# Norm of the second MLP in the transposed layout, with statistics taken behind the first MLP and sent to all partitions by transfers

## The chip, the cores and the metric

The kernel runs on 1 core of one Trainium2 chip. The metric is device time of one execution in microseconds: before the change the median of three runs is 1674.12 us (1673.66 to 1674.39). The engines are TensorE (PE in the rows; PEld is its weight load), VectorE (DVE), ScalarE (ACT), GpSimd (POOL) and SyncE (SP), which here only issues transfers.

## The reference

A linear attention, a token-and-channel mixer and a normalized MLP follow each other; batch 8, 576 tokens, width 512 (8 heads of 64), hidden widths 256 (tokens), 1536 and 2048 (channels).

```python
q_s = softmax(q, over d); k_s = softmax(k, over tokens)
x = q_s @ (k_s.T @ v)                    # per head, heads side by side: [8, 576, 512]
h = relu(x.T @ w_tok1) @ w_tok2          # mixing over tokens
u = x + h.T
y = u + relu(u @ w_ch1) @ w_ch2          # first MLP, 512 -> 1536 -> 512
mu, var = mean(y), mean((y - mu) ** 2)   # per token, over the 512 channels
xn = (y - mu) / sqrt(var + 1e-6) * g_ln
out = y + relu(xn @ w2_ch1) @ w2_ch2     # second MLP, 512 -> 2048 -> 512
```

The MLPs' weights are float64 in memory and are decoded on the chip; the other inputs are float32.

## The kernel before

The 4608 tokens are worked in nine blocks of 512: blocks 0 to 7 hold the first 512 tokens of a batch, block 8 holds the last 64 of all eight. Each float32 operand of the MLPs is split into two parts, hi and lo, which the matmul reads as float32r, and a product is three matmuls (`PASSES`). The kernel has two halves:

- `Phase1(j)`: the first MLP of block j, in the transposed layout (channels on partitions, 512 tokens as columns). Per hidden chunk f of 12: `L1` (line 684), 12 matmuls of 512 columns, then `L2` of the chunk two steps earlier (line 701), 12 more. The attention of the next batch (`Unit`) runs between them. At the end, `finish` makes yT (4 x 128 channels by 512 tokens, buffer `y` of `main`), and `y_store` turns it back, 128 tokens at a time: 4 transposes on TensorE, a copy by ScalarE, a transfer to `y_dram`.
- `Phase2(j)`: the second MLP of block j. Per hidden chunk f of 16: `L1` (line 829) with xT, then `L2` (line 844). `Norm(j)` prepares xT while the block before is worked: it loads the rows, takes mean and variance per token (lines 768, 770), the inverse root in six small instructions, subtracts and scales (793), turns the result on TensorE (804, `px`), and writes hi (809, ScalarE) and lo (810, VectorE) of xT, with g as a factor per partition. `load` fetches the rows again for the residual, and `finish` adds and stores them.

The weights of the second MLP are decoded and split by VectorE, ScalarE and GpSimd (lines 100 to 130) in the last two blocks of the first half and the first block of the second; `loads.until` puts that work ahead of the matmuls that need it.

The order on each engine is the order of the code: `later(n, fn)` puts a piece of work n turns ahead, and `tick()` ends a turn. A chunk has four turns in the first half (one in the middle and one at the end of `L1` and of `L2`) and two in the second, so a turn there is one half step of 12 matmuls. `LAG = 2` and two buffers of `ps_hid` stand between a chunk's `L1`, its relu (ScalarE, then VectorE) and its `L2`.

Tiles of a pool lie behind each other in the order of their first use. In `main` they are ident (512 bytes of a partition), gT (16), the 12 weight tiles, h, yT, stages, xT (u), t, and then the small ones st6, mv, ve, r0 and r1 (96, 32, 16, 16, 16). The pool `att` lies behind `main`; when it is released, `w2pool` takes its place, with a stage, the weight tiles of hidden chunks 0 to 3 of the second MLP and one buffer `y` for the rows that `Norm` works on. Starts are rounded up to 32 bytes; `main` starts at a multiple of 64.

Of the kernel before, what the change touches and what calls it, by code (L numbers as in the profile page):

```python
# [16 lines left out]
P = 128  # L17
# [7 lines left out]
def kernel(  # L25
# [23 lines left out]
    nc = tc.nc  # L49
    B, H, S, D = q.shape  # L50
    DM = H * D
# [6 lines left out]
    NT = B * S  # L58
# [9 lines left out]
    BLK = 512  # L68
    NB = NT // BLK
    CT = BLK // P  # L70
    LAG = 2

    main = ctx.enter_context(tc.tile_pool(name="main", bufs=1))
# [234 lines left out]
    def later(n, fn):  # L308
        ticks.setdefault(now[0] + n, []).append(fn)
# [318 lines left out]
    def y_store(j, c):  # L628
        pt = psum("py")
        for kk in range(KD):  # L630
            nc.tensor.transpose(  # L631
                out=pt[:, kk * P:(kk + 1) * P], in_=yT_t[j][:, kk, c * P:(c + 1) * P],
                identity=ident,
            )
        if w2p:
            if c == 0:
                yn_t[j] = w2p[0].tile([P, CT, DM], F32, tag="y", name="yn")
            yn = yn_t[j][:, c]
        else:
            yn = main.tile([P, DM], F32, tag="t", bufs=2, name="yn")  # L640
        nc.scalar.activation(out=yn, in_=pt[:, 0:DM], func=AF.Copy)
        if j < B:
            dst = y_dram[j * S:j * S + S0, :].rearrange("(p c) d -> c p d", c=NC)[c]
            nc.scalar.dma_start(out=dst, in_=yn)
            return
        for i in range(P // R):
            b = c * (P // R) + i
            nc.scalar.dma_start(out=y_dram[b * S + S0:(b + 1) * S, :], in_=yn[i * R:(i + 1) * R])

    def load_ends():  # L650
        u_t[B] = main.tile([P, 2, KD, BLK], F32R, tag="u", bufs=2, name="u")
# [4 lines left out]
    class Phase1:  # L656
# [51 lines left out]
        def finish(self):  # L708
            if self.f1 < NF1:
                t = [main.tile([P, 512], F32, tag="t", bufs=2, name="part") for _ in range(2)]  # L710
                x = att.tile([P, 2, 512], F32, tag="qx", name="part")
                for dd, o in enumerate((t[0], t[1], x[:, 0], x[:, 1])):
                    nc.scalar.activation(out=o, in_=self.acc[dd], func=AF.Copy)
                for dd in range(2):
                    nc.sync.dma_start(out=part_dram[:, dd], in_=t[dd])
                nc.sync.dma_start(out=part_dram[:, 2:4], in_=x)
                return
            yT_t[self.j] = main.tile([P, KD, BLK], F32, tag="y", bufs=1, name="yT")
            yT, u = yT_t[self.j], u_t[self.j]
            for dd in range(KD):  # L720
                x = self.part[dd // 2][:, dd % 2] if self.f0 else u[:, 0, dd].bitcast(F32)
                nc.vector.tensor_tensor(out=yT[:, dd], in0=self.acc[dd], in1=x, op=ALU.add)  # L722
            def add(c):
                x = slice(c * P, (c + 1) * P)
                nc.gpsimd.tensor_tensor(  # L725
                    out=yT[:, :, x], in0=yT[:, :, x], in1=u[:, 1, :, x].bitcast(F32), op=ALU.add
                )

            for c in range(CT):
                if self.f0 == 0:  # L730
                    later(2 * c if self.j > 1 else 0, lambda c=c: add(c))
                later((5, 8, 12, 15)[c] if self.j < B - 1 else 5 + 2 * c, lambda c=c: y_store(self.j, c))
# [1 line left out]

    ln_t = {}

    def load_y(j, pool):
        y = pool.tile([P, CT, DM], F32, tag="y", name="y")
        src = y_dram[j * BLK:(j + 1) * BLK, :]
        nc.sync.dma_start(out=y, in_=src.rearrange("(p c) d -> p c d", c=CT))  # L740
        return y

    class Norm:
        def __init__(self, j):
            self.j = j

        def start(self, at, turns=12):
            def call(fn, i):
                return lambda: fn(i)

            later(at, self.load)
            for i in range(CT // 2):
                later(at + 4 + i, call(self.stats, i))
                later(at + 9 + i, call(self.hat, i))
            later(at + 6, self.root)
            later(at + 8, self.rstd)
            for kk in range(KD):
                later(at + turns + kk + kk // 2, call(self.turn, kk))

        def load(self):  # L760
            self.y = load_y(self.j, w2p[0])

        def stats(self, i):
            if i == 0:
                self.st = main.tile([P, CT, 6], F32, tag="st6", name="st6")
                self.mv = main.tile([P, CT, 2], F32, tag="mv", name="mv")
            for c in range(2 * i, 2 * i + 2):
                nc.vector.bn_stats(out=self.st[:, c], in_=self.y[:, c])
            for c in range(2 * i, 2 * i + 2):
                nc.vector.bn_aggr(out=self.mv[:, c], in_=self.st[:, c])  # L770

        def root(self):
            self.ve = main.tile([P, CT], F32, tag="ve", name="ve")
            self.r = main.tile([P, CT], F32, tag="r0", name="r0")
            nc.vector.tensor_scalar(
                out=self.ve, in0=self.mv[:, :, 1], scalar1=1e-6, scalar2=None, op0=ALU.add
            )
            later(1, lambda: nc.scalar.activation(out=self.r, in_=self.ve, func=AF.Sqrt))

        def rstd(self):  # L780
            ve, r0 = self.ve, self.r
            r1 = main.tile([P, CT], F32, tag="r1", name="r1")
            nc.vector.reciprocal(out=r0, in_=r0)
            nc.vector.tensor_tensor(out=r1, in0=r0, in1=r0, op=ALU.mult)
            nc.vector.tensor_tensor(out=r1, in0=r1, in1=ve, op=ALU.mult)
            nc.vector.tensor_scalar(
                out=r1, in0=r1, scalar1=-0.5, scalar2=1.5, op0=ALU.mult, op1=ALU.add
            )
            nc.vector.tensor_tensor(out=r0, in0=r0, in1=r1, op=ALU.mult)

        def hat(self, i):
            for c in range(2 * i, 2 * i + 2):
                nc.vector.tensor_scalar(
                    out=self.y[:, c], in0=self.y[:, c], scalar1=self.mv[:, c, 0:1],
                    scalar2=self.r[:, c:c + 1], op0=ALU.subtract, op1=ALU.mult,
                )

        def turn(self, kk):
            if kk == 0:
                self.xT = main.tile([P, 2, KD, BLK], F32R, tag="u", bufs=2, name="xT")  # L800
                ln_t[self.j] = self.xT
            pt = psum("px")
            for c in range(CT):
                nc.tensor.transpose(  # L804
                    out=pt[:, c * P:(c + 1) * P],
                    in_=self.y[:, c, kk * P:(kk + 1) * P], identity=ident,
                )
            g = gT[:, kk:kk + 1]
            nc.scalar.activation(out=self.xT[:, 0, kk], in_=pt, func=AF.Copy, scale=g)
            nc.vector.scalar_tensor_tensor(  # L810
                out=self.xT[:, 1, kk], in0=pt, scalar=g, in1=self.xT[:, 0, kk].bitcast(F32),
                op0=ALU.mult, op1=ALU.subtract,
            )

    class Phase2:
# [1 line left out]
            self.j, self.f1 = j, NF2  # L817

        def load(self):
            self.y = load_y(self.j, main)  # L820

        def L1(self, f, mid):
            xT = ln_t[self.j]
# [25 lines left out]
                    )  # L849

        def finish(self):
            y = self.y
            dst = out[self.j * BLK:(self.j + 1) * BLK, :].rearrange("(p c) d -> p c d", c=CT)
            for c in range(CT):
                nc.vector.tensor_tensor(out=y[:, c], in0=self.acc[c], in1=y[:, c], op=ALU.add)  # L855
                if self.j == NB - 1:
                    nc.sync.dma_start(out=dst[:, c], in_=y[:, c])
            if self.j < NB - 1:
                nc.gpsimd.dma_start(out=dst, in_=y)  # L859

    with tc.manual_schedule():
        spare += [
# [65 lines left out]
        for j in range(NB):  # L928
            o = Phase2(j)
            steps += [(o, f) for f in range(NF2)]  # L930

# [19 lines left out]
        for o, f in steps:  # L951
            if isinstance(o, Phase1):
# [4 lines left out]
                if f == 0:  # L957
# [3 lines left out]
                    elif o.j == B - 1:  # L961
# [13 lines left out]
                        for n in range(5, 29):  # L975
                            later(n, lambda: loads.pump(2))
                        later(20, load_ends)
                    elif o.j == NB - 1:
                        Norm(0).start(18, 15)
                if o.j <= 1:  # L980
                    loads.until(len(tok) + 4 * (f // 2) + 2)
            else:
                if o.j == 0:
                    loads.until(4 * (f // 2) + 2)
                if f == 0:
                    later(16, o.load)
                    if o.j + 1 < NB:
                        Norm(o.j + 1).start(14 if o.j == 0 else 8)
# [44 lines left out]
```

## Time and profile before

| | |
|---|---|
| median of three runs | 1674.12 us |
| the profiled execution, its span | 1673.57 us, 1671.8 us |
| TensorE, its weight load, busy | 98%, 83% |
| VectorE, ScalarE, GpSimd busy | 39%, 25%, 19% |
| mean DMA rate | 63 GB/s |

The first half lasts to about 855 us of the span, the second to the end. Starts in a timeline are in us from the span's start. Matmuls are pipelined, so the busy time of one is more than its distance from the next; the pace is read from starts.

### The profile page before, as it was taken

How to read it: one execution, taken by the hardware profiler on the slowest of the kernel's cores; microseconds unless marked ns; L12 is line 12 of the kernel's file. 1: busy time of each engine (PE TensorE's matmuls, PEld its weight loads, DVE VectorE, ACT ScalarE, POOL GpSimd, SP SyncE). 2: the span in 40 equal slices, each digit the busy share in tenths (PEclk: the TensorE clock that was granted, in tenths of full speed). 3: DMA queues.
4: the chain of work that ended last, by engine and by line, in shares of the span. 5: the costliest groups of instructions: out<-in, count | busy, mean ns of one | idle time of the engine just before them, and what ended most of it. 6: DMA issues, size and time to landing. Idle time of an engine off the chain costs nothing.

```text
span 1671.8 us, 20195 instructions
## 1 busy us (share of the span) xinstructions
PE 1642.0 (98%) x8136; PEld 1380.9 (83%) x8136; DVE 644.3 (39%) x1290; ACT 410.1 (25%) x824; POOL 318.5 (19%) x244
## 2 busy tenths in 40 slices
PE   5999999999999999999999999999999999999998
PEld 4888888888888888888888888888888888888887
DVE  6875434344333434353557621222223131222211
ACT  4663333323232323321222211111111111111110
POOL 5743522232232313221223200000000000000000
PEclk9999999999999999999999999999999999999999
DMA  8552312121121212133225210101010101010010
GB/s 230 126 159 75 87 49 69 49 53 51 42 68 28 76 36 69 28 107 114 88 86 173 76 44 25 51 25 51 25 51 25 51 17 60 0 69 8 5 46 26
DMA packets 122062, 105.39 MB, mean 63 GB/s; under 512 B 92976, under 2 KB 101424, under 8 KB 118512
## 3 DMA queue, kind: packets, MB, share of 16 engines
q1 hardware_dynamic: 115568, 86.27, 17.9%
q10 hardware_dynamic: 5248, 9.44, 1.6%
q0 software_dynamic: 1152, 8.39, 1.2%
q8 instruction: 64, 1.05, 0.3%
q14 instruction: 30, 0.25, 0.0%
HBM read 82.05 MB, written 22.02 MB: 62 GB/s over the span
## 4 chain that ended last, share of the span: by engine, by line
PE 94%; DVE 2%; POOL 1%; issue 1%; ACT 1%; DMA 1%; SPq 0%; POOLq 0%; DVEq 0%; ACTq 0%
PE ph L829 24%; PE acc L844 24%; PE ph L684 17%; PE acc L701 17%; PE pu L601 4%; PE pg L538 3%; PE pk L514 2%; PE py L631 1%; PE px L804 1%; PE pq L559 1%; PE pq L586 1%; DMA rawq<-in_q 0%; DVE spare L138 0%; DVE dt L108 0%; POOL yT L725 0%
## 5 line engine op out<-in xcount | busy, mean ns | idle before, releaser
L142 DVE SCALAR_TENSOR_TENSOR h<-ph,h 128x512 fp32r<-128x512 f32 x252 | 174.0, 691 | 708.8 <-ACT h L141 708.7
L829 PE MATMUL ph<-xT,w 128*128 128x512 f32 x1728 | 420.2, 392 | 0.0
L844 PE MATMUL acc<-w,h 128*128 128x512 f32 x1728 | 420.0, 392 | 0.0
L829 PEld LDWEIGHTS ph<-xT,w 128*128 128x128 f32 x1728 | 323.0, 188 | 70.5 <-POOL w L130 0.2
L844 PEld LDWEIGHTS acc<-w,h 128*128 128x128 f32 x1728 | 322.9, 188 | 68.9
L141 ACT ACTIVATE h<-ph 128x512 fp32r<-128x512 f32 x252 | 150.5, 597 | 770.7 <-PE ph L829 587.0
L684 PE MATMUL ph<-u,w 128*128 128x512 f32 x1296 | 324.7, 395 | 0.0
L701 PE MATMUL acc<-h,w 128*128 128x512 f32 x1296 | 323.7, 394 | 0.0
L701 PEld LDWEIGHTS acc<-h,w 128*128 128x128 f32 x1296 | 237.1, 188 | 46.7
L684 PEld LDWEIGHTS ph<-u,w 128*128 128x128 f32 x1296 | 236.8, 188 | 46.7 <-DVE u L621 0.4
L859 POOL DMA_DIRECT2D out<-y x8 | 4.4, 556 | 635.8 <-DVE y L855 635.8
L467 POOL TENSOR_TENSOR qt<-rawq,qm 128x640 f32<-128x640 f32 x24 | 30.3, 1261 | 241.0 <-PE pt L461 95.5
L130 POOL TENSOR_TENSOR w<-t,w 128x512 fp32r<-128x512 f32 x32 | 41.9, 1310 | 152.8 <-ACT w L129 152.8
L538 PE MATMUL pg<-w,qn 128*128 128x256 f32 x480 | 63.8, 285 | 3.4 <-ACT w L137 3.4
L538 PEld LDWEIGHTS pg<-w,qn 128*128 128x128 f32 x480 | 62.0, 193 | 6.0 <-ACT w L137 3.7
L601 PE MATMUL pu<-w,hs 128*128 128x288 f32 x384 | 61.4, 295 | 0.0
L601 PEld LDWEIGHTS pu<-w,hs 128*128 128x128 f32 x384 | 54.4, 188 | 0.3 <-ACT hs L141 0.2
L138 DVE TENSOR_TENSOR qT<-pq,qT 128x512 fp32r<-128x512 f32 (+1 forms) x48 | 22.0, 458 | 76.1 <-ACT qT L137 76.1
L725 POOL TENSOR_TENSOR yT<-yT,u 128x512 f32<-128x512 f32 x32 | 43.0, 1359 | 37.9 <-DVE yT L722 37.9
L482 POOL TENSOR_TENSOR kt<-rawk,kb 128x640 f32<-128x640 f32 x24 | 38.1, 1587 | 40.8 <-ACT kb L478 40.8
L138 POOL TENSOR_TENSOR qn<-qt,qn 128x640 fp32r<-128x640 f32 x24 | 38.0, 1582 | 32.7 <-ACT qn L137 30.9
L129 ACT ACTIVATE w<-t 128x512 fp32r<-128x512 f32 x32 | 20.3, 633 | 97.0 <-DVE t L121 94.6
(140 smaller groups left out, 1243.3 us busy)
## 6 DMA issues: line engine op xcount, KB each, us to landing
y<-y_dram SPq DMA_DIRECT2D x18, 1024.0 KB, 4.8
st<-in_moe_w_ch SPq DMA_DIRECT2D x31, 512.0 KB, 3.8
vt<-in_v SPq DMA_DIRECT2D x64, 128.0 KB, 2.9
y_dram<-yn ACTq DMA_DIRECT2D x32, 256.0 KB, 2.4
out<-y POOLq DMA_DIRECT2D x8, 1024.0 KB, 4.1
rawk<-in_k SPq DMA_DIRECT2D x54, 128.0 KB, 2.8
rawq<-in_q SPq DMA_DIRECT2D x27, 256.0 KB, 3.1
stage<-in_moe_w_ch SPq DMA_DIRECT2D x10, 512.0 KB, 3.8
```

Of the source, the lines that this page charges most:

```text
L130: nc.gpsimd.tensor_tensor(out=lo, in0=x, in1=hi.bitcast(F32), op=ALU.subtract)
L138: engine.tensor_tensor(out=lo, in0=x, in1=hi.bitcast(F32), op=ALU.subtract)
L141: nc.scalar.activation(out=hi, in_=x, func=AF.Relu)
L142: nc.vector.scalar_tensor_tensor(out=lo, in0=x, scalar=0.0, in1=hi.bitcast(F32), op0=ALU.max, op1=ALU.subtract)
L482: nc.gpsimd.tensor_tensor(out=self.kt, in0=self.kr, in1=kb.to_broadcast([P, NC + 1, 2, D]), op=ALU.subtract,)
L538: nc.tensor.matmul(out=pg[:, 0:T], lhsT=self.qn[:, x, c], rhs=w1[:, y, c, :], start=(n == 0), stop=(n == len(terms) - 1),)
L601: nc.tensor.matmul(out=pu[:, 0:HN], lhsT=l, rhs=r, start=(n == 0), stop=(n == len(terms) - 1))
L684: nc.tensor.matmul(out=ps, lhsT=w[:, x, kk, fo:fo + P], rhs=u[:, y, kk], start=(n == 0), stop=(n == 3 * KD - 1),)
L701: nc.tensor.matmul(out=self.acc[dd], lhsT=w[:, x, f % 2, dd * P:(dd + 1) * P], rhs=h[:, y], start=(f == self.f0 and n == 0), stop=(f == se ...
L725: nc.gpsimd.tensor_tensor(out=yT[:, :, x], in0=yT[:, :, x], in1=u[:, 1, :, x].bitcast(F32), op=ALU.add)
L829: nc.tensor.matmul(out=ps, lhsT=w[:, x, kk, fo:fo + P], rhs=xT[:, y, kk], start=(n == 0), stop=(n == 3 * KD - 1),)
L844: nc.tensor.matmul(out=self.acc[c], lhsT=h[:, x, c * P:(c + 1) * P], rhs=w[:, y, f % 2], start=(f == 0 and n == 0), stop=(f == self.f1 - 1 ...
```

## The change

Statistics are taken in `y_store`, from the copy that ScalarE has just made, and kept in `mr`. yT is stored a second time as it stands (`yT_dram`). `Root` makes the inverse roots for seven blocks at once near the end of the first half and for the other two in block 0 of the second; it turns the table of means and inverse roots with one transpose each time and stores it to `mr_dram`. `Norm` then loads yT and, for half of the tokens at a time, mean and inverse root sent to all 128 partitions by a transfer; VectorE subtracts, GpSimd multiplies, and hi and lo of xT are made from that without TensorE. All scratch tensors have a block as their first dimension. The second half goes through the blocks in the order 0 to 6, 8, 7.

```diff
-    y_dram = dram.tile([NT, DM], F32, name="y_dram")
+    y_dram = dram.tile([NB, P, CT, DM], F32, name="y_dram")
+    yT_dram = dram.tile([NB, P, KD, BLK], F32, name="yT_dram")
+    mr_dram = dram.tile([NB, 2 * BLK], F32, name="mr_dram")
+
+    mr = main.tile([P, NB, 2, CT], F32, name="mr")
...
+        nc.scalar.dma_start(out=y_dram[j, :, c], in_=yn)
+        st = main.tile([P, 6], F32, tag="st6", bufs=2, name="st6")
+        nc.vector.bn_stats(out=st, in_=yn)
+        nc.vector.bn_aggr(out=mr[:, j, :, c], in_=st)
...
+            later(8, lambda: nc.sync.dma_start(out=yT_dram[self.j], in_=yT))
...
+    class Root:
...
+        def start(self, at):
+            for n, fn in zip((0, 1, 2, 3), (self.root, self.rstd, self.turn, self.store)):
+                later(at + 2 * n, fn)
...
+        def turn(self):
+            n = (self.j1 - self.j0) * 2 * CT
+            pm = psum("pm")
+            nc.tensor.transpose(
+                out=pm[:n, 0:P],
+                in_=mr[:, self.j0:self.j1].rearrange("p j x c -> p (j x c)"), identity=ident,
+            )
+            self.rows = main.tile([P, P], F32, tag="mrr", name="mrr")[:n]
+            nc.scalar.activation(out=self.rows, in_=pm[:n, 0:P], func=AF.Copy)
+
+        def store(self):
+            dst = mr_dram[self.j0:self.j1].rearrange("j (x p) -> (j x) p", p=P)
+            nc.sync.dma_start(out=dst, in_=self.rows)
...
+            later(at, self.load)
+            for i in range(2):
+                later(at + 4 * i, call(self.load_b, i))
+                later(at + 4 * i + 4, call(self.hat, i))
+            for kk in range(KD):
+                later(at + turns + kk + kk // 2, call(self.turn, kk))
+
+        def load(self):
+            self.y = w2p[0].tile([P, KD, BLK], F32, tag="y", name="yT")
+            nc.sync.dma_start(out=self.y, in_=yT_dram[self.j])
+
+        def load_b(self, i):
+            self.b = w2p[0].tile([P, 2, HB], F32, tag="mrb", name="mrb")
+            src = mr_dram[self.j].rearrange("(x n) -> x n", x=2)[:, i * HB:(i + 1) * HB]
+            nc.sync.dma_start(out=self.b, in_=src.partition_broadcast(P))
+
         def hat(self, i):
...
+            y = self.y[:, :, i * HB:(i + 1) * HB]
+            mu, r = (self.b[:, x:x + 1].to_broadcast([P, KD, HB]) for x in range(2))
+            nc.vector.tensor_tensor(out=y, in0=y, in1=mu, op=ALU.subtract)
+            nc.gpsimd.tensor_tensor(out=y, in0=y, in1=r, op=ALU.mult)
...
-            pt = psum("px")
-            for c in range(CT):
-                nc.tensor.transpose(
-                    out=pt[:, c * P:(c + 1) * P],
-                    in_=self.y[:, c, kk * P:(kk + 1) * P], identity=ident,
-                )
-            g = gT[:, kk:kk + 1]
-            nc.scalar.activation(out=self.xT[:, 0, kk], in_=pt, func=AF.Copy, scale=g)
+            g, y = gT[:, kk:kk + 1], self.y[:, kk]
+            nc.scalar.activation(out=self.xT[:, 0, kk], in_=y, func=AF.Copy, scale=g)
...
+        ORDER = [*range(B - 1), B, B - 1]
+        for j in ORDER:
...
+                        Root(0, B - 1).start(30)
                     elif o.j == NB - 1:
                         Norm(0).start(18, 15)
...
+                    later(18, o.load)
+                    if o.j == 0:
+                        Root(B - 1, NB).start(26)
+                    if o.j != ORDER[-1]:
+                        Norm(ORDER[ORDER.index(o.j) + 1]).start(15 if o.j == 0 else 8)
```

On TensorE in the second half, before, around the turn of a block (a row is a place in the engine's order; acc and ph are the sums of `L2` and `L1`, px the turned rows):

```order
1094 L829 MATMUL ph_8551<-xT,w 128x512 x12
1095 L804 MATMUL px<-ident,y 128x128 x4
1096 L844 MATMUL acc_8311<-w,h 128x512 x3
1097 L844 MATMUL acc_8312<-w,h 128x512 x3
1098 L844 MATMUL acc_8313<-w,h 128x512 x3
1099 L844 MATMUL acc_8314<-w,h 128x512 x3
1100 L804 MATMUL px<-ident,y 128x128 x4
1101 L829 MATMUL ph_8594<-xT,w 128x512 x12
```

and the same place now:

```order
1092 L842 MATMUL ph_8640<-xT,w 128x512 x12
1093 L857 MATMUL acc_8383<-w,h 128x512 x3
1094 L857 MATMUL acc_8384<-w,h 128x512 x3
1095 L857 MATMUL acc_8385<-w,h 128x512 x3
1096 L857 MATMUL acc_8386<-w,h 128x512 x3
1097 L842 MATMUL ph_8670<-xT,w 128x512 x12
```

The transposes between the half steps are gone, and nothing stands in their place. On VectorE, before, near the end of block 0 of the second half (lines 100 to 121 decode weights, L142 is the lo part of h, L810 that of xT):

```order
903 L121 SCALAR_TENSOR_TENSOR t<-stage_6575,t 128x512
904 L810 SCALAR_TENSOR_TENSOR xT<-px,gT,xT 128x512
905 L142 SCALAR_TENSOR_TENSOR h<-ph_8117,h 128x512
906 L100 TENSOR_SCALAR st<-st 128x512
907 L108 TENSOR_SCALAR t<-st 128x512
```

and now, with the small instructions of the second table:

```order
962 L126 SCALAR_TENSOR_TENSOR t<-stage_6656,t 128x512
963 L822 SCALAR_TENSOR_TENSOR xT<-yT,gT,xT 128x512
964 L147 SCALAR_TENSOR_TENSOR h<-ph_8186,h 128x512
965 L762 RECIPROCAL mr<-mr 128x2x4
966 L763 TENSOR_TENSOR r_8202<-mr 128x8
967 L764 TENSOR_TENSOR r_8202<-r_8202,ve 128x8
968 L765 TENSOR_SCALAR r_8202<-r_8202 128x8
969 L768 TENSOR_TENSOR mr<-mr,r_8202 128x2x4
970 L822 SCALAR_TENSOR_TENSOR xT<-yT,gT,xT 128x512
```

Behind the lo part of ph_8186 five small instructions have come in, for which TensorE's transpose of the table waits. That transpose stands behind the next group, ph_8235:

```order
1021 L842 MATMUL ph_8186<-xT,w 128x512 x12
1022 L857 MATMUL acc_7717<-w,h 128x512 x3
1023 L857 MATMUL acc_7718<-w,h 128x512 x3
1024 L857 MATMUL acc_7719<-w,h 128x512 x3
1025 L857 MATMUL acc_7720<-w,h 128x512 x3
1026 L842 MATMUL ph_8235<-xT,w 128x512 x12
1027 L773 MATMUL pm<-ident,mr 16x128
```

So two half steps lie between the group and the transpose. On SyncE's queue a block of the second half had two loads of 1 MB before (`y<-y_dram`, all blocks in one row, with the last decoded weights ahead and the last stores behind):

```order
263 L163 DMA st<-in_moe_w_ch 128x2x512
264 L163 DMA stage_6575<-in_moe_w_ch 128x2x512
265 L183 DMA st<-in_moe_w_ch 128x1024 x2
266 L740 DMA y<-y_dram 128x2048 x15
267 L857 DMA out<-y 128x512 x4
```

and has now, behind the store of the second table:

```order
279 L188 DMA st<-in_moe_w_ch 128x1024 x2
280 L782 DMA mr_dram<-mrr 16x128
281 L803 DMA yT<-yT_dram 128x2048
282 L808 DMA mrb<-mr_dram 128x2x256 x2
283 L833 DMA y<-y_dram 128x2048
284 L803 DMA yT<-yT_dram 128x2048
```

Two broadcasts have come between the two loads of a block, the second of them with a wait for GpSimd.

## Rows read from the trace of the kernel before

**Rows 1.** The page: busy shares, granted clock by slice, and the chain that ended last.

```profile
PE 1642.0 (98%) x8136; PEld 1380.9 (83%) x8136; DVE 644.3 (39%) x1290; ACT 410.1 (25%) x824; POOL 318.5 (19%) x244
...
PEclk9999999999999999999999999999999999999999
...
PE 94%; DVE 2%; POOL 1%; issue 1%; ACT 1%; DMA 1%; SPq 0%; POOLq 0%; DVEq 0%; ACTq 0%
```

**Rows 2.** Waits of TensorE: line, releaser, us in total, times, longest.

```profile
PE pt L433 <- DMA spare<-in_k: 5.1, 1, 5.1
PE pt L433 <- DMA rawk<-in_k: 4.5, 1, 4.5
...
```

**Rows 3.** Groups by line, the transposes: busy us, mean ns of one, idle before.

```profile
L804 PE MATMUL px<-ident,y 128*128 128x128 f32 x144 | 21.6, 272 | 0.0
```

**Rows 4.** Timeline of TensorE, one block's turn: start, us, engine, line, count.

```profile
1001.91 2.88 PE L829 MATMUL ph<-xT,w 128*128 128x512 f32 x12
1004.63 0.60 PE L804 MATMUL px<-ident,y 128*128 128x128 f32 x4
1004.99 2.99 PE L844 MATMUL acc<-w,h 128*128 128x512 f32 x12
...
1020.09 2.88 PE L829 MATMUL ph<-xT,w 128*128 128x512 f32 x12
1022.81 2.43 PE L844 MATMUL acc<-w,h 128*128 128x512 f32 x10
```

**Rows 5.** Timeline of TensorE, the first chunks of block 1.

```profile
946.80 2.95 PE L829 MATMUL ph<-xT,w 128*128 128x512 f32 x12
...
960.63 2.96 PE L844 MATMUL acc<-w,h 128*128 128x512 f32 x12
963.43 2.96 PE L829 MATMUL ph<-xT,w 128*128 128x512 f32 x12
...
985.59 2.88 PE L829 MATMUL ph<-xT,w 128*128 128x512 f32 x12
```

**Rows 6.** Timeline of TensorE, matmuls of the attention: early and in the first half.

```profile
36.72 1.87 PE L538 MATMUL pg<-w,qn 128*128 128x256 f32 x15
38.42 0.46 PE L570 MATMUL pq<-spare,qn 128*128 128x128 f32 x4
...
413.48 0.96 PE L601 MATMUL pu<-w,hs 128*128 128x288 f32 x6
414.27 1.55 PE L684 MATMUL ph<-u,w 128*128 128x512 f32 x6
```

**Rows 7.** Groups by line, elementwise work: busy us, mean ns, idle before and releaser.

```profile
L725 POOL TENSOR_TENSOR yT<-yT,u 128x512 f32<-128x512 f32 x32 | 43.0, 1359 | 37.9 <-DVE yT L722 37.9
...
L768 DVE BATCH_NORM_STATS2 st<-y 128x6 f32<-128x512 f32 x36 | 22.8, 676 | 4.9 <-DMA y<-y_dram 4.9
L855 DVE TENSOR_TENSOR y<-acc,y 128x512 f32<-128x512 f32 x36 | 22.5, 682 | 4.8 <-PE acc L844 4.8
L770 DVE BATCH_NORM_AGGREGATE mv<-st 128x2 f32<-128x6 f32 x36 | 5.4, 173 | 0.0
```

**Rows 8.** Timeline of all engines, near the end of block 0 of the second half.

```profile
925.88 0.68 DVE L115 SCALAR_TENSOR_TENSOR t<-st,t 128x512 uint32<-128x512 uint32 x1
...
928.04 1.29 POOL L130 TENSOR_TENSOR w<-t,w 128x512 fp32r<-128x512 f32 x1 [4.32 <-ACT w L129]
928.20 1.68 DVE L115 SCALAR_TENSOR_TENSOR t<-st,t 128x512 uint32<-128x512 uint32 x1
...
932.15 2.89 PE L844 MATMUL acc<-w,h 128*128 128x512 f32 x12
...
935.62 0.68 DVE L142 SCALAR_TENSOR_TENSOR h<-ph,h 128x512 fp32r<-128x512 f32 x1
```

**Rows 9.** DMA issues: transfer, queue, count, KB each, median us to landing.

```profile
y<-y_dram SPq DMA_DIRECT2D x18, 1024.0 KB, 4.8
...
rawq<-in_q SPq DMA_DIRECT2D x27, 256.0 KB, 3.1
```

More of the change, by code (lines that the diff above doesn't have):

```diff
@@ L70 @@
     CT = BLK // P
+    HB = BLK // 2
     LAG = 2
@@ L641, in y_store @@
         nc.scalar.activation(out=yn, in_=pt[:, 0:DM], func=AF.Copy)
[L642 to L648, printed above, removed]
+        nc.scalar.dma_start(out=y_dram[j, :, c], in_=yn)
+        st = main.tile([P, 6], F32, tag="st6", bufs=2, name="st6")
+        nc.vector.bn_stats(out=st, in_=yn)
+        nc.vector.bn_aggr(out=mr[:, j, :, c], in_=st)
     def load_ends():
@@ L751, in start @@
             later(at, self.load)
[L752 to L756, printed above, removed]
+            for i in range(2):
+                later(at + 4 * i, call(self.load_b, i))
+                later(at + 4 * i + 4, call(self.hat, i))
             for kk in range(KD):
@@ L760, in load @@
         def load(self):
[L761 to L776, printed above, removed]
-            )
[L778 to L789, printed above, removed]
@@ L791, in hat @@
-        def hat(self, i):
[L792 to L796, printed above, removed]
+            self.y = w2p[0].tile([P, KD, BLK], F32, tag="y", name="yT")
[4 more added lines that the diff above has]
+            nc.sync.dma_start(out=self.b, in_=src.partition_broadcast(P))
@@ L819, in load @@
         def load(self):
-            self.y = load_y(self.j, main)
+            self.y = main.tile([P, CT, DM], F32, tag="y", name="y")
+            nc.sync.dma_start(out=self.y, in_=y_dram[self.j])
         def L1(self, f, mid):
@@ L851, in finish @@
         def finish(self):
-            y = self.y
-            dst = out[self.j * BLK:(self.j + 1) * BLK, :].rearrange("(p c) d -> p c d", c=CT)
+            y, last = self.y, self.j == ORDER[-1]
+            if self.j < B:
+                dst = out[self.j * S:self.j * S + S0, :].rearrange("(p c) d -> p c d", c=CT)
+                dst = [(slice(0, P), dst)]
+            else:
+                dst = out.rearrange("(b s) d -> s b d", s=S)[S0:S]
+                n = P // R
+                dst = [
+                    (slice(i * R, (i + 1) * R), dst.rearrange("s (c i) d -> i s c d", i=n)[i])
+                    for i in range(n)
+                ]
             for c in range(CT):
                 nc.vector.tensor_tensor(out=y[:, c], in0=self.acc[c], in1=y[:, c], op=ALU.add)
[L856 to L859, printed above, removed]
+                if last:
+                    for p, x in dst:
+                        nc.sync.dma_start(out=x[:, c], in_=y[p, c])
+            if not last:
+                for p, x in dst:
+                    nc.gpsimd.dma_start(out=x, in_=y[p])
     with tc.manual_schedule():
@@ L927 @@
             steps += [(o, f) for f in range(o.f0, o.f1)]
-        for j in range(NB):
+        ORDER = [*range(B - 1), B, B - 1]
+        for j in ORDER:
             o = Phase2(j)
@@ L985 @@
                 if f == 0:
-                    later(16, o.load)
-                    if o.j + 1 < NB:
-                        Norm(o.j + 1).start(14 if o.j == 0 else 8)
+                    later(18, o.load)
[3 more added lines that the diff above has]
+                        Norm(ORDER[ORDER.index(o.j) + 1]).start(15 if o.j == 0 else 8)
             ps, n = o.L1(f, tick)
```

28 lines of the change are left out of this document (21 added, 7 removed).

## The prediction

> **What bounds the kernel now.** I read the page's busy shares and its chain first, then who TensorE waits for, then TensorE's timeline in the second half. The reader is to see that TensorE is busy for 98% of the span and carries 94% of the chain [rows 1], and that it waits for named releasers only in the front of the kernel, where q, k and v arrive: the two longest waits are 5.1 and 4.5 us [rows 2], and both are on line 433, which runs for the first eight units alone. From the middle on, the end is set by the number of TensorE instructions times their pace, and by nothing else. So an edit counts if it takes TensorE work away, changes TensorE's pace, or makes TensorE wait. Work of VectorE, ScalarE, GpSimd and the queues counts only through the third.
>
> **The transposes that go.** Each of the nine blocks of the second MLP has its normalized rows turned on TensorE: 144 transposes, 36 groups of four [rows 3]. Their busy time doesn't say what they cost, since matmuls overlap, so I take it from starts. Without a transpose, the twelve matmuls of a half step follow each other in 2.72 us (1020.09 to 1022.81) [rows 4]. The stretch from 1001.91 to 1020.09 has six such half steps and the four groups of one block: 18.18 us, where six alone take 6 x 2.72 = 16.32. One block's turn therefore costs 1.86 us, of which about 0.35 a group are the transposes (1004.63 to the next start, 1004.99) and the rest is the slower run-in of the matmuls behind them. Nine blocks: 9 x 1.86 = 16.7 us, all on the bounding engine. This is the term I am surest of.
>
> **What TensorE gets instead.** Two transposes of the table of means and deviations (line 773), one with 56 rows and one with 16. Each is at most a group of four: 1.86 / 4 = 0.47 us, and at least a quarter of the 0.35. Both together 0.2 to 0.9; I take 0.5.
>
> **A term the diff doesn't name: where the tiles lie.** The first half steps of each second-MLP block are slower with no transpose near: 960.63 to 963.43 is 2.80 us, where 2.72 is usual [rows 5]. From 946.80 to 985.59 there are 14 half steps in 38.79 us; 14 x 2.72 = 38.08, so 0.71 us a block, 6.4 us over nine. The slow half steps of both matrices are those of hidden chunks 0 to 3, whose weights lie in the pool `w2pool`; all other weights lie in `main`. In `main` the identity (512 bytes) and gT (16, rounded up to 32) come first, so every weight, xT and h tile starts 32 bytes past a multiple of 64; the small tiles at the end of `main` add 96 + 4 x 32 = 224, so `w2pool` starts on a multiple of 64. A slow matmul thus pairs a tile at 0 with one at 32, a fast one two tiles at 32. The change puts mr (9 x 2 x 4 x 4 = 288 bytes, 32 past a multiple of 64) behind gT, and its small tiles at the end come to 64 + 160 + 160 + 512 = 896, a multiple of 64. Everything then starts on a multiple of 64, `w2pool` too. How fast is a pair at 0 and 0? The attention's tiles are such pairs: six matmuls of 288 columns take 413.48 to 414.27, 132 ns each, 12 above the 120 of 288 columns at 2.4 GHz, the clock that is granted from the first slices on [rows 1, 6]. A pair at 32 and 32 takes 2720 / 12 = 226.7, 13 above the 213.3 of 512 columns; the mixed pair 233.3, 20 above. So I read the excess as that of a mismatch, which the change removes: between 0 and 6.4 us, or a loss if the reading is wrong (below). I take 6.4.
>
> The Trainium skill ("SBUF — State Buffer", section "Specifications (TRN2)") gives SBUF lines of 16 bytes, and a penalty for crossing to a new one. By that rule a start 32 bytes further on changes nothing, and this term would be zero (rival 1). The rows above show 0.08 us a half step between two places, and no run so far shows that it is the start and not the region that makes it.
>
> **VectorE, ScalarE, GpSimd.** Statistics move from the second half to the copies behind the first MLP: 36 bn_stats at 676 ns and 36 bn_aggr at 173 [rows 7], 0.85 us each pair, 3.4 a block on a VectorE that is 39% busy [rows 1]. Each waits for ScalarE's copy of that tile. Behind it stands the lo part of h, which TensorE needs four half steps (10.9 us) later; that covers it. Per block of the second MLP, VectorE loses four subtract-and-scale instructions and gets two subtractions of 1024 columns. The nearest rows are 682 ns for 512 columns of two inputs (line 855) and 680 for two inputs from SBUF (line 115) [rows 7, 8], so 1.4 us each. GpSimd gets two multiplications of 1024 columns: line 725 does 512 in 1359 ns, so 2.7 us. In a steady block the first half of the tokens is worked at turn 12 and the second at turn 16 of 32, and ScalarE starts on xT at turn 20. A turn is a half step there. From turn 16 there are 4 x 2.72 = 10.9 us for 1.4 + 2.7 = 4.1. Nothing of this is on the path.
>
> **The transfers.** A block's rows are written a second time (1 MB), loaded transposed (1 MB; 4.8 us for such a load [rows 9]) and joined by two broadcasts of 256 KB (3.1 us for the nearest load of that size, 4.8 for the upper end). On SyncE's queue the second broadcast waits for GpSimd's first product, since both use one buffer, and y for the residual is queued behind it. That delays y by the same 4.1 us at most; it is needed at the block's end, 14 turns (38 us) later. In the first half the extra store waits for GpSimd's last add, at a place where the loads ahead of it have already waited for later work of GpSimd. No cost.
>
> **The two places with little room.** Both are at the change of halves, where weights are still being decoded. (a) Block 0: its first subtraction stands on VectorE eleven turns ahead of the first xT (in the first half a turn is a quarter step, 1.4 us), but blocks VectorE until row load and broadcast have landed, and again for the second broadcast: two waits of up to 4.8 us, against a cover of three half steps (8.2 us) before TensorE needs the buffer that VectorE holds. (b) The second table: the transposition stands two half steps (5.44 us) behind the group whose lo part the last five small VectorE instructions follow. In the profile a lo part there starts 3.5 us after its group (932.15 to 935.62) and takes 0.68; five small ones add about 1: 5.1 us of 5.44. GpSimd's longer products can hold VectorE up: a step on line 115 takes 0.68 us alone and 1.68 where GpSimd works [rows 8]. Two such holds of up to 2.7 us make the upper end, 5 us; the lower end is 0. I take 1 us for both places.
>
> The Trainium skill ("SBUF — State Buffer", "Who interferes with whom") says that a VectorE instruction with two SBUF inputs and a GpSimd instruction that reads SBUF exclude each other for the whole instruction; the 1.68 agrees. By it alone each product would hold VectorE for its full 2.7 us wherever they meet, and the sum would have the 5 us in place of 1.
>
> **The sum.** -16.7 + 0.5 - 6.4 + 1.0 = -21.6 us on the profiled execution's 1673.57 us (span 1671.8 and 1.8 around it), which lies 0.55 below the median of 1674.12. On the median: 1652.5 us. Its own range is 1650 to 1657 (waits 0 to 5, the two transposes 0.2 to 0.9).
>
> **Rivals.**
> 1. The slow half steps are slow for another reason (region of memory, not start): the 6.4 stays. 1674.12 - 16.7 + 0.5 + 1 = 1659. For it: no row here has 512 columns at 0 and 0.
> 2. Pairs at 0 and 0 are faster than any now. For it: fifteen matmuls of 256 columns at 0 and 0 take 36.72 to 38.42, 113 ns each, 7 above 106.7 [rows 6]. With 7 above 213.3 for 512 columns, the 5184 matmuls of a pair at 32 and 32 would gain 6.4 ns and the 864 mixed ones 13: 33 + 11 = 44 us in place of the 6.4, and 1615. Against it: the 288-column rows, at 12. Halfway, 1634.
> 3. The other side: a start at 0 is itself what costs, 20 above the columns or more. The 512-column rows alone would bear this too, as each slow pair has a tile at 0. The 5184 matmuls that now have 226.7 would get 233.3: + 34 us, and 1674.12 + 34 - 15.2 = 1693. It decides from 15.2 / 5184 = 2.9 ns a matmul on. Against it stand the 132 ns above.
> 4. The transposes go, but TensorE waits in their place: (a) or (b) at several times their bound, or each block's two broadcasts land late. A steady block has 10.9 - 4.1 = 6.8 us of room, so it would take loads of over 11 us. With 1.2 us a block and 5 at the change of halves: 1653 + 11 + 4 = 1668.
>
> **Chances.** Forecast 0.57, rival 1 0.18, rival 2 0.12, rival 3 0.06, rival 4 0.07. The range from 1636 to 1661 holds the first two and the weaker part of the third. A measurement can tell about 0.2% (3.3 us) from no change. Faster by more: the forecast, rivals 1 and 2 and most of 4: 0.91. Slower: rival 3 with little else, 0.06. Within: 0.03.
>
> **What would show it.** Right: no transposes of px, no gap in their place, half steps of 2.72 us at all turns of a second-MLP block, so a block of 32 x 2.72 = 87.0 us; VectorE's statistics early. Wrong: half steps of 2.80 at hidden chunks 0 to 3 (rival 1), of 2.65 or less everywhere (2), of 2.80 everywhere (3), or TensorE idle before xT or line 773 (4).

## The result, and the profile after

The changed kernel takes 1659.34 us (median of four runs, 1658.92 to 1659.97), against 1674.24 us (1673.66 to 1674.39) for the kernel before in the same comparison: a ratio of 0.9912, 95% interval 0.9899 to 0.9926. That is 14.9 us faster, where 21.6 was forecast. The time lies in the wide range, 1636 to 1661, and on the figure of rival 1, whose reason turned out to be wrong. The forecast's own range, 1650 to 1657, doesn't hold it.

The page of the changed kernel: busy shares, the granted clock by slice, and the chain that ended last.

```profile
PE 1624.8 (98%) x7994; PEld 1365.8 (82%) x7994; DVE 650.0 (39%) x1230; ACT 408.5 (25%) x819; POOL 363.9 (22%) x263
...
PEclk9999999999999999999999999999999999999999
...
PE 90%; DVE 4%; DMA 1%; issue 1%; POOL 1%; ACT 1%; SPq 1%; DVEq 0%; POOLq 0%; ACTq 0%
```

Against [rows 1] TensorE has 142 instructions less (144 transposes gone, two added) and 17.2 us less of busy time. It still bounds the kernel. In the chain DVE now has 4%, where it had 2%.

Who TensorE waits for in the changed kernel (us in total, times, longest); the first two answer to [rows 2], the last two are new.

```profile
PE pt L438 <- DMA spare<-in_k: 5.4, 1, 5.4
PE pt L438 <- DMA rawk<-in_k: 4.7, 1, 4.7
...
PE ph L686 <- DVE h L147: 0.9, 1, 0.9
...
PE pm L773 <- DVE mr L768: 0.5, 1, 0.5
```

Here is where the time went, from the starts of the blocks in both traces. Seven steady blocks of the second MLP fell from 89.63 to 87.74 us each (-1.89). Its first block fell from 91.53 to 89.91. The last block of the first half, which prepares the first normalised rows and so gets rid of one turn too, fell by 0.59 only, and the block ahead of it, which holds the first table, grew by 0.75. The last block of all grew by 0.1. Five blocks of the first half, ahead of these two, became 0.4 shorter in all; why is open. The front grew by 0.75, but it differs by that much between runs of kernels that are equal there, so it isn't put down to the change. Together this is -14.2 us, by which the two profiled spans differ (1671.8 and 1657.6); the medians are 14.9 apart.

TensorE's timeline in a steady block of the changed kernel, first chunks (above "...") and a place from chunk 4 on in another block (below); it answers to [rows 4, 5].

```profile
1121.14 2.96 PE L842 MATMUL ph<-xT,w 128*128 128x512 f32 x12
1123.94 2.92 PE L857 MATMUL acc<-w,h 128*128 128x512 f32 x12
1126.70 2.96 PE L842 MATMUL ph<-xT,w 128*128 128x512 f32 x12
1129.49 2.92 PE L857 MATMUL acc<-w,h 128*128 128x512 f32 x12
...
1000.76 2.88 PE L842 MATMUL ph<-xT,w 128*128 128x512 f32 x12
1003.48 2.88 PE L857 MATMUL acc<-w,h 128*128 128x512 f32 x12
```

No transposes stand between the half steps at 1000.76, and a start follows the one before by 2.72 us. But from 1121.14 a pair of half steps still takes 5.56 us (1121.14 to 1126.70) instead of 5.44. The slow half steps of [rows 5] did not go.

The elementwise groups of the changed kernel that answer to [rows 7]: busy us, mean ns, idle before.

```profile
L649 DVE BATCH_NORM_STATS2 st<-yn 128x6 f32<-128x512 f32 x36 | 24.7, 687 | 21.1 <-ACT yn L646 21.1
...
L813 DVE TENSOR_TENSOR yT<-yT,mrb 128x1024 f32<-128x1024 f32 x18 | 24.1, 1340 | 6.0 <-DMA mrb<-mr_dram 6.0
L814 POOL TENSOR_TENSOR yT<-yT,mrb 128x1024 f32<-128x1024 f32 x18 | 43.9, 2436 | 252.5 <-issue 180.3 <-DVE yT L813 72.2
```

The sizes were about as estimated (1.4 us for VectorE's subtraction, 2.7 for GpSimd's product; 676 ns for the statistics). The broadcasts land 5.1 us behind their issue in the list of DMA issues (median of 18), above the 3.1 to 4.8 taken for them from [rows 9].

Last, all engines of the changed kernel at the one place where the first normalised block makes TensorE wait.

```profile
832.68 1.23 DVE L813 TENSOR_TENSOR yT<-yT,mrb 128x1024 f32<-128x1024 f32 x1 [2.21 <-DMA mrb<-mr_dram]
...
833.99 2.78 POOL L814 TENSOR_TENSOR yT<-yT,mrb 128x1024 f32<-128x1024 f32 x1 [3.80 <-DVE yT L813]
834.55 2.77 DVE L126 SCALAR_TENSOR_TENSOR t<-st,t 128x512 uint32<-128x512 uint32 x1
...
837.35 0.63 ACT L134 ACTIVATE w<-t 128x512 fp32r<-128x512 f32 x1 [9.70 <-DVE t L126]
837.89 1.07 ACT L146 ACTIVATE h<-ph 128x512 fp32r<-128x512 f32 x2
...
838.50 0.69 DVE L147 SCALAR_TENSOR_TENSOR h<-ph,h 128x512 fp32r<-128x512 f32 x1 [1.18 <-ACT h L146]
...
839.25 2.14 PE L686 MATMUL ph<-u,w 128*128 128x512 f32 x8 [0.93 <-DVE h L147]
```

It is read from the bottom up: TensorE needs a PSUM tile that VectorE's line 147 frees. Line 147 stands behind ScalarE's line 146, that behind ScalarE's line 134, and that behind VectorE's line 126, which takes 2.77 us beside GpSimd's product where it takes 0.69 alone.

### The profile page after: what moved, and what is told of

Same layout as the page of the kernel before. It is cut to its first block, busy times and chain, and to the rows that moved or that the text cites. A ratio compares the mean times of both kernels' runs of the same rounds, so it can differ in the third digit from the quotient of the medians.

```text
span 1657.6 us, 19945 instructions
## 1 busy us (share of the span) xinstructions
PE 1624.8 (98%) x7994; PEld 1365.8 (82%) x7994; DVE 650.0 (39%) x1230; ACT 408.5 (25%) x819; POOL 363.9 (22%) x263
## 4 chain that ended last, share of the span: by engine, by line
PE 90%; DVE 4%; DMA 1%; issue 1%; POOL 1%; ACT 1%; SPq 1%; DVEq 0%; POOLq 0%; ACTq 0%
PE ph L842 24%; PE acc L857 24%; PE ph L686 16%; PE acc L703 16%; PE pu L606 4%; PE pg L543 3%; PE pk L519 2%; PE py L636 1%; PE pq L564 1%; PE pq L591 1%; DVE t L120 1%; DMA mrb<-mr_dram 1%; DVE t L126 1%; DMA rawq<-in_q 0%; DVE spare L143 0%
## 5 line engine op out<-in xcount | busy, mean ns | idle before, releaser
L814 POOL TENSOR_TENSOR yT<-yT,mrb 128x1024 f32<-128x1024 f32 x18 | 43.9, 2436 | 252.5 <-issue 180.3
```

Source lines behind the costliest of these rows:

```text
L814: nc.gpsimd.tensor_tensor(out=y, in0=y, in1=r, op=ALU.mult)
```

## Experiments

**The transposes put back.** On TensorE alone, into a PSUM tile that nothing reads:

```
+            pt = psum("px")
+            for c in range(CT):
+                nc.tensor.transpose(
+                    out=pt[:, c * P:(c + 1) * P], in_=y[:, c * P:(c + 1) * P], identity=ident,
+                )
```

> The changed kernel with the four 128x128 transposes of each turned Norm put back on TensorE; their result is not used. Theory 'the gain is TensorE's own time for the transposes': each block gets its 1.86 to 1.89 us back, about 1675 us, level with the kernel before. Rival 'the gain came from waits that the transposes had caused': clearly less comes back, 1660 to 1668 us.

Measured: 1675.34 us, ratio to the kernel before 1.0007 (0.9997 to 1.0016). A steady block is 89.58 us again, 1.84 more than in the changed kernel. TensorE's timeline of this kernel shows the groups back at the half steps:

```profile
1006.35 0.60 PE L823 MATMUL px<-ident,yT 128*128 128x128 f32 x4
1006.70 2.99 PE L862 MATMUL acc<-w,h 128*128 128x512 f32 x12
1009.53 0.60 PE L823 MATMUL px<-ident,yT 128*128 128x128 f32 x4
```

So the gain is TensorE's own time for the transposes and for the matmuls behind them (from 1006.70 to 1009.53 it is 2.83 us instead of 2.72).

**Other weights for the slow chunks.** The weights of hidden chunks 4 to 7, whose tiles lie in `main`, are read in chunks 0 to 3 of eight of the nine blocks of the second MLP (all but block 0); so the product is another one.

```
-            w, fo = wa2[f // 2], (f % 2) * P
+            w, fo = wa2[f // 2 + 2 if f < 4 and self.j else f // 2], (f % 2) * P
```

and the same for `wb2`.

> In blocks 1 to 7 of each half where the condition holds, hidden chunks 0 to 3 read the weights of chunks 4 to 7, whose tiles lie low in SBUF, in place of their own (so the output differs from the reference; count and shape of the matmuls stay). Theory 'place of the weights': the half steps of 2.80 us in chunks 0 to 3 become 2.72 as in chunks 4 to 7, 0.64 to 0.71 us a block, about 5 us less in all: near 1654 us. Theory 'turn in the block or work beside it': half steps stay 2.80 and the time stays at 1659 us.

Measured: 1653.41 us (ratio 0.9873, 0.9856 to 0.9889). Each of the eight blocks is 0.70 us shorter; TensorE's timeline at the first chunks:

```profile
1119.59 2.88 PE L842 MATMUL ph<-xT,w 128*128 128x512 f32 x12
1122.31 2.88 PE L857 MATMUL acc<-w,h 128*128 128x512 f32 x12
```

All starts of these chunks are 2.72 us apart. It is the tiles, then, and not the turn in the block or the work that runs beside it. That left two readings: the tiles lie high in memory, or their start doesn't fit their partner's.

**A map of the memory.** Twelve tiles from 20 to 217 KB, all pairs as stationary and moving operand, nothing beside.

> A measurement by itself: nothing of the reference is computed, the output is one constant tile. Twelve tiles of 128x512 fp32r at rising addresses of SBUF (a at 20 KB of a partition, b 60, c 100, d 140, e 160, f 172, g 178, h 184, i 190, j 198, k 208, l 217), and 24 matmuls of 512 columns for each pair of a tile as stationary operand and a tile as moving one, nothing else running beside. Theory 'the address itself': a pair with one of the upper tiles takes about 233 ns a matmul and a pair of lower ones about 227, with a boundary between 182 and 185 KB. Theory 'two regions in one pair': pairs of two lower and pairs of two upper tiles take 227, mixed ones 233. Theory 'not the place at all' (the turn in the block, or what runs beside): all pairs take the same to within 1 ns.

Measured, from TensorE's timeline of this kernel (pair of the lowest tile with itself and with the highest):

```profile
13.23 5.60 PE L42 MATMUL paa<-ata 128*128 128x512 f32 x24
18.67 5.60 PE L42 MATMUL pab<-atb,ata 128*128 128x512 f32 x24
...
73.07 5.60 PE L42 MATMUL pal<-atl,ata 128*128 128x512 f32 x24
```

The second series starts 5.44 us behind the first, and so does every other: 226.7 ns a matmul, and no pair differs by as much as 0.1 ns. The height in memory costs nothing. This seems to contradict the experiment before it, until one looks at what the twelve tiles have in common: all start on a multiple of 1024 bytes.

**Both operands from the upper tiles.** In the first multiplication of chunks 0 to 3 (the same eight blocks) the moving operand is a weight tile of the upper region instead of xT.

```
-                        out=ps, lhsT=w[:, x, kk, fo:fo + P], rhs=xT[:, y, kk],
+                        out=ps, lhsT=w[:, x, kk, fo:fo + P],
+                        rhs=wb2[1 - f // 2][:, y, kk % 2] if f < 4 and self.j else xT[:, y, kk],
```

> In the later blocks the first multiplication of hidden chunks 0 to 3 takes as its moving operand a weight tile that lies high in SBUF, as its stationary one does, in place of xT, which lies low (the output differs from the reference; count and shape of the matmuls stay). Theory 'two regions in one pair': these half steps become 2.72 us, those of the second multiplication stay 2.80. Theory 'the address itself': they stay 2.80, or rise to about 2.88 if both operands pay.

Measured: one run of 1659.16 us. TensorE's timeline:

```profile
1122.34 2.89 PE L842 MATMUL ph<-w 128*128 128x512 f32 x12
1125.07 2.89 PE L858 MATMUL acc<-w,h 128*128 128x512 f32 x12
...
1133.26 2.89 PE L842 MATMUL ph<-w 128*128 128x512 f32 x12
1135.99 2.96 PE L858 MATMUL acc<-w,h 128*128 128x512 f32 x12
1138.79 2.92 PE L842 MATMUL ph<-w 128*128 128x512 f32 x12
1141.54 2.95 PE L858 MATMUL acc<-w,h 128*128 128x512 f32 x12
```

Two upper tiles together are fast: 2.73 us from 1122.34 to 1125.07 and from 1133.26 to 1135.99. An upper weight tile with the low h stays slow (1135.99 to 1138.79, 2.80), and the fast pair behind it starts slowly (2.75). A block is 0.24 us shorter; the whole time hides it, since this run's front and first half were 1.9 us longer up to the change of halves. So it takes a pair of unlike tiles, as the prediction had it. In the compiled program the lower weights, xT and h start at 192 modulo 256; the upper weights (186176 and further by multiples of 8192) start at 64. Modulo 64 both are 0, and there the prediction had stopped.

**128 bytes of room.** The changed kernel with one unused tile:

```
                         bufs[:] = [w2pool.tile([P, 512, 2], U32, name="stage3")]
+                        w2pool.tile([P, 32], U32, name="pad")
```

> The changed kernel, with 128 unused bytes of a partition ahead of the weight tiles of hidden chunks 0 to 3, nothing else. All weights, xT and h now start at 448 bytes modulo 512; before this the four upper tiles started at 320 and their partners at 448 (equal modulo 64 and 128, not modulo 256). Theory 'starts of the two operands of a matmul must agree over a longer stretch than 64 bytes': the half steps of 2.80 us in chunks 0 to 3 become 2.72, 0.64 to 0.71 us a block over nine blocks, about 6 us less: 1653 us. Theory 'high address': half steps stay 2.80, 1659 us.

Measured: 1652.71 us (ratio 0.987, 0.9855 to 0.9885). TensorE's timeline at the same chunks as above:

```profile
1118.92 2.88 PE L842 MATMUL ph<-xT,w 128*128 128x512 f32 x12
1121.64 2.88 PE L857 MATMUL acc<-w,h 128*128 128x512 f32 x12
1124.36 2.88 PE L842 MATMUL ph<-xT,w 128*128 128x512 f32 x12
```

Starts are 2.72 us apart everywhere, a steady block takes 87.04 us (32 x 2.72), and the nine blocks give back 6.3 us (0.67 in the first, 0.70 in each of the others). Only the starts of that pool's tiles moved, so the start is shown to be the cause.

**Which starts agree.** A sweep by itself.

> A measurement by itself: nothing of the reference is computed, the output is one constant tile. Sixty series of 48 matmuls of 512 columns, the stationary operand read from 0, 64, 128 or 320 bytes behind a multiple of 512, the moving one from 0 to 1024 bytes behind one (in the names of the tiles digits are written a to j, so pgexbci is stationary 64, moving 128). Theory 'starts must agree': 226.7 ns a matmul where the two differ by a multiple of 256 or 512, 231 to 235 ns where they differ by 64, 128 or 192 bytes (and by 32, as in the kernel before); the differences at which it is fast give the stretch. Theory 'it takes more than the starts': 226.7 ns for all.

Measured, TensorE's timeline with the stationary operand at 0 (`pa` + x + the moving one's bytes):

```profile
13.08 11.04 PE L44 MATMUL paxa<-mv,st 128*128 128x512 f32 x48
23.96 11.28 PE L44 MATMUL paxbg<-mv,st 128*128 128x512 f32 x48
35.08 11.37 PE L44 MATMUL paxdc<-mv,st 128*128 128x512 f32 x48
46.28 11.15 PE L44 MATMUL paxge<-mv,st 128*128 128x512 f32 x48
57.27 11.37 PE L44 MATMUL paxjg<-mv,st 128*128 128x512 f32 x48
68.48 11.36 PE L44 MATMUL paxbci<-mv,st 128*128 128x512 f32 x48
79.68 11.40 PE L44 MATMUL paxbga<-mv,st 128*128 128x512 f32 x48
...
102.11 11.09 PE L44 MATMUL paxcfg<-mv,st 128*128 128x512 f32 x48
113.04 11.17 PE L44 MATMUL paxdca<-mv,st 128*128 128x512 f32 x48
```

From start to start over 48: moving operand at 0: 226.7 ns; at 16: 231.7; 32: 233.3; 64: 229.0; 96: 233.5; 128: 233.3; 256 (`paxcfg`): 227.7, with its first matmuls up to 236 and the later half at 226.7. The other stationary starts (64, 128, 320) repeat it: wherever the two differ by a multiple of 256 the later half runs at 226.7. A moving operand 64 behind the stationary one takes 228.9, less than the 231 to 235 expected there; one 192 behind takes 233.3, so the distance doesn't count alike both ways. The start itself (0, 64, 128 or 320) makes no difference.

**64 bytes of room**, as a dose: the same line with `[P, 16]`.

> The changed kernel with 64 bytes ahead of the upper weight tiles in place of 128. They start at 128 modulo 256, xT and h at 192. By the series measured apart, a moving operand 64 behind the stationary one takes 228.9 ns and one 192 behind 233.3: the first multiplication of chunks 0 to 3 (moving xT 64 behind) should fall from some 232.5 to 229 ns, 0.3 us a block, and the second one (moving weights 192 behind h) stay at 233. About 2.5 us less in all, 1656.8 us, so that the cost is one-sided. If the distance counted alike in both directions, both would fall: 1655 us. If only agreement counts: 1659 us.

Measured: 1658.07 us (ratio 0.9904, 0.9889 to 0.9919); a steady block is 0.14 us shorter, not 0.3. TensorE's timeline:

```profile
1126.27 2.91 PE L842 MATMUL ph<-xT,w 128*128 128x512 f32 x12
1129.02 2.88 PE L857 MATMUL acc<-w,h 128*128 128x512 f32 x12
...
1134.49 2.96 PE L857 MATMUL acc<-w,h 128*128 128x512 f32 x12
1137.29 2.96 PE L842 MATMUL ph<-xT,w 128*128 128x512 f32 x12
1140.08 2.96 PE L857 MATMUL acc<-w,h 128*128 128x512 f32 x12
```

Beside fast neighbours the first multiplication takes 2.75 us (1126.27), as the sweep says. Between slow ones it stays at 2.79 (1137.29): the same pair is fast or slow by its neighbours. That fits the missing half of the expected gain. Why the pace carries over is open.

**The kernel before with 32 bytes of room** (`[P, 8]` at the same place; upper weights from 128 to 160 modulo 256, where the others are).

> The kernel before, with 32 unused bytes ahead of the upper weight tiles, so that they, the lower ones, xT and h all start at 160 bytes modulo 256; before this the upper ones started at 128. If the slow half steps of the kernel before come from the same cause as those of the changed one, they become 2.72 us, 0.70 to 0.72 us a block over nine blocks: 1674.2 - 6.4 = 1667.8 us. If not, 1674.2 us.

Measured: 1667.95 us (ratio 0.9962, 0.9948 to 0.9977). TensorE's timeline of this kernel, at the first chunks of a block:

```profile
1124.72 2.88 PE L829 MATMUL ph<-xT,w 128*128 128x512 f32 x12
1127.44 2.88 PE L844 MATMUL acc<-w,h 128*128 128x512 f32 x12
```

Starts are 2.72 us apart here too, and each of the nine blocks is 0.69 to 0.71 us shorter, 6.3 together. The slow half steps of [rows 5] had the same cause.

**The two waits at the change of halves.** First the product of the first two normalised blocks on VectorE:

```
-            nc.gpsimd.tensor_tensor(out=y, in0=y, in1=r, op=ALU.mult)
+            engine = nc.vector if self.j < 2 else nc.gpsimd
+            engine.tensor_tensor(out=y, in0=y, in1=r, op=ALU.mult)
```

> The changed kernel, with the multiplication by the deviation's inverse of the first two normalised blocks on VectorE in place of GpSimd. Theory 'GpSimd's 2.79 us beside VectorE stretch the 0.69-us reading of PSUM to 2.77 us and so hold ScalarE and the hidden tile': VectorE's stretched line and TensorE's wait of 0.93 us in the first half's last block go, about 1.3 us less: 1658.0 us. Rival 'it is the late transfer of the means that holds the block': VectorE's 1.2 us more for each product come at the same place, the wait stays and the time stays within 0.3 us of 1659.3.

Measured: 1657.7 us (ratio 0.9901, 0.9885 to 0.9918, which overlaps that of the changed kernel; the traces tell them apart). The last block of the first half is 1.27 us shorter, the next 0.18, all others are equal to 0.03. All engines of this kernel, at the place shown above:

```profile
830.71 1.23 DVE L813 TENSOR_TENSOR yT<-yT,mrb 128x1024 f32<-128x1024 f32 x1 [0.47 <-DMA mrb<-mr_dram]
831.97 1.22 DVE L815 TENSOR_TENSOR yT<-yT,mrb 128x1024 f32<-128x1024 f32 x1
...
833.83 0.69 DVE L126 SCALAR_TENSOR_TENSOR t<-st,t 128x512 uint32<-128x512 uint32 x1
```

Line 126 is back at 0.69 us and TensorE's wait is gone. (The expectation calls the held line a reading of PSUM; by the rows it is line 126, which reads st and t, both in SBUF.) VectorE's own product takes 1.22 us, less than the 2.08 us of hold that it ends. The second broadcast also lands earlier for VectorE (0.47 us of waiting instead of 2.21), since its buffer comes free earlier. Both come of GpSimd's product, which is so shown to be behind TensorE's wait; how much the hold has in it and how much the late broadcast, this run doesn't part.

Then the table's transpose two turns later: `zip((0, 1, 3, 4), ...)` in place of `(0, 1, 2, 3)`.

> The changed kernel, with the transpose of the sums table and its store one step (two ticks) later after the reciprocals. Theory 'TensorE waits for VectorE's reciprocals because the transpose comes 0.5 us too early': the wait of 0.46 us and the restart after it go in the first half, 0.5 to 0.75 us less, 1658.7 us. Rival 'the store lands later, and the first normalised block with it': the gain is lost again in the block after, 1659.3 us or more.

Measured: 1658.37 us (ratio 0.9905, 0.989 to 0.992; again the traces tell more). The block with the first table is 0.63 us shorter, the next 0.17, and the wait on line 773 is gone. The later store costs no more than 0.04 us, in the first block of the second MLP.

**All three together.**

> The three edits that gained by themselves in one kernel: 128 bytes ahead of the upper weight tiles, the multiplication of the first two normalised blocks on VectorE, the transpose of the sums table one step later. If each takes away its own loss (6.45, 1.45 and 0.80 us between the same places of the traces), they add up: 8.7 us below the changed kernel's 1659.3, 1650.6 us. If the second and third cure the same wait, about 1 us less is gained: 1651.5 us.

Measured: 1651.49 us (ratio 0.9865, 0.9849 to 0.9882). By the traces it is 1.95 us shorter than the kernel with 128 bytes of room alone in the three blocks concerned (0.57, 1.23 and 0.15), where the two edits gave 2.25 one by one. The 0.3 between them say little: the last block of the first half differs by up to 0.34 us from the changed kernel's in a run whose edit doesn't touch it (the one with other weights). It is 22.5 us below the kernel before in this comparison (1673.95), and close to the 1652.5 that the prediction had for the change itself.

## Why the prediction was right, and where it was wrong

**The transposes: right.** 1.86 us a block were read from starts; blocks that lost nothing else got 1.89 shorter, and 1.84 came back with the transposes.

**The places of the tiles: the step that failed.** The prediction took 6.4 us for "a mismatch, which the change removes"; 0 came. That a pair of unlike starts is slow was right, and so was the price (0.67 to 0.71 a block measured, 0.71 predicted). The step that failed is "everything then starts on a multiple of 64" as a reason for agreement: the rows had only one distance, 32 bytes, and a multiple of 64 was taken for enough. The change turned a distance of 32 bytes into one of 128, and the sweep has 233.3 ns for both. Had the addresses been compared modulo more than 64, the distance of 128 would have been seen.

A row of before could have warned. The prediction took the attention's 132 ns [rows 6] as those of a matching pair, "12 above" the columns' 120, since a matching pair of 512 columns is 13 above. But the excess isn't fixed: 256 columns take 113.3 ns in the same rows, half of the 226.7 of 512, so it grows with the columns. At that pace 288 columns are 127.5 ns, and at the slow pace (233.3) 131.2; the 131.7 measured is the slow one. By their addresses the moving operand of those six matmuls starts at 128 modulo 256 and the stationary one at 0, so that they are a mismatch themselves, though both are 0 modulo 64.

The Trainium skill's 16-byte lines ("SBUF — State Buffer", "Specifications (TRN2)") gave zero for this term as the prediction applied them, and zero came. But that a start moved by whole lines changes nothing, which the prediction drew from them, isn't borne out: a start 128 bytes further on gave 6.3 us, and a distance of 16 bytes, one whole line, costs 5 ns a matmul.

**Rival 1** had the time, 1659, through "region of memory". The map refutes the region: 226.7 ns at all heights. A forecast can hit a number by the wrong cause. **Rivals 2 and 3** (starts at 0 faster, or dearer) are refuted by the sweep: equal starts give 226.7 at each of the four values tried (0, 64, 128, 320). Rival 2 came of the same reading: its 113 ns for 256 columns are the pace of 226.7, not a faster one. **Rival 4** is refuted for the steady blocks, which are 87.74 us, 32 x 2.72 and the slow half steps' 0.70; at the change of halves TensorE did wait.

**The waits.** Place (a) came as described, with GpSimd's product holding a VectorE line for 2.77 us; it cost about 1.3 us by the run that took the product away, where 1 was taken for both places together. The Trainium skill's rule that such a pair excludes each other for the whole instruction ("SBUF — State Buffer", "Who interferes with whom") agrees with that row; by it alone the sum would have had 5 us, and only one such hold reached TensorE. Place (b) cost nothing that the waits show: the second table's transpose starts without one.

**The tables' transposes: mis-sized.** 0.5 us was taken for both as TensorE's own time. The block of the first table grew by 0.75, of which 0.63 went with a later transpose: that was a wait, at the table that the prediction hadn't looked at, and 0.12 is left. In the trace ScalarE's table load stands ahead of its square root there (1.28 us), and VectorE's five small instructions end 0.15 us before the transpose starts. Two turns lie between these and the transpose at both tables, but in the first half a turn is a quarter step, so they are 2.7 us there and 5.44 at the second table. **No cost** was right for VectorE's and GpSimd's work and the transfers in steady blocks, where nothing but the half steps is left.

## What to carry to other kernels

When a change adds or removes tiles, list the start of each matmul's two operands in the compiled program and compare them modulo 256; a pad of 32 or 128 bytes was worth 6.3 us here, beside the rewrite's 14.9. This was measured with float32r operands and 512 columns. A regularity read from one distance in the trace gives the price of that distance, not the rule: measure a sweep before a term rests on it. Where the bounding engine is full, what counts is its instructions and their pace; what other engines do costs only where the bounding engine's next tile has less room than one of their holds, here at the change of halves.

## What the runs showed that was not expected

- The pace of a 512-column matmul depends on the distance between the starts of its two operands: 226.7 ns at multiples of 256 bytes, 228.9 with the moving one 64 behind, 231.7 at 16, 232 to 235 at the others that were tried. What in the chip makes it so no run shows.
- Matching pairs don't reach 226.7 at once: after a series of another distance single matmuls of up to 236 ns come first, and 1 to 10 pass in the sweep before the pace is even. Single matmuls look alike behind a group of transposes (231, 236, 228, 233 and 231 ns, then 227, behind one group of the kernel before); that it is the same thing is not shown.
- At the fast pace the time of these float32r matmuls goes with their columns: 113.3 ns for 256 [rows 6], 226.7 for 512. An excess over some figure is to be compared by the column, not by the matmul.
